# Threshold attention into an ELU feed-forward block: idle transposes and step order in the first stage, and the place of the weight conversion in the second

## The chip, the core and the metric

The kernel runs on one core of one Trainium2 chip. The metric is the device time of one execution in microseconds. The kernel before takes 1376.89 us, the median of three runs (1376.81 to 1378.41).

A core has five engines that work side by side, each through its own list of instructions in order, and wait for one another by semaphores: TensorE (PE in the profile; its weight loads are shown apart as PEld), VectorE (DVE), ScalarE (ACT), GpSimd (POOL) and SyncE (SP), which issues the transfers. TensorE writes its results to PSUM; the operands of the others lie in SBUF or PSUM.

## What is computed

Attention with a threshold, for 8 sequences of 8 heads with 576 positions of 64 numbers, and behind it a feed-forward block with the ELU function:

```python
scores = scale * np.matmul(q, k.transpose(0, 1, 3, 2))
thresh = np.max(scores, axis=-1, keepdims=True) - tau
scores = np.where(scores >= thresh, scores, -1000000000.0)
scores = scores - np.max(scores, axis=-1, keepdims=True)
attn = np.exp(scores)
attn = attn / (np.sum(attn, axis=-1, keepdims=True) + 1e-09)
x = np.matmul(attn, v)            # then heads side by side: 4608 x 512
h = x @ w_in                      # 512 -> 2048
g = np.where(h > 0.0, h, np.exp(np.minimum(h, 0.0)) - 1.0)
return g @ w_out                  # 2048 -> 512
```

q, k and v come as 32-bit numbers. The two weight matrices come as 64-bit numbers, and the kernel turns them into 32-bit ones itself, from the two 32-bit halves of each.

## The kernel before

**Steps.** Two heads make a pair; a sequence has four pairs, and the kernel 32. A pair is worked in five steps i = 0 to 4. Steps 0 to 3 each take 128 query rows of both heads; step 4 takes the last 64 rows of both heads as one block of 128. Steps are numbered through as n: n = 0 to 19 are the first sequence, and n = 20 begins the second.

**One step.** TensorE makes the scores of a head as two products of 288 columns (line 236, tile `sc`). VectorE takes the maximum of each row (276 in the first stage, 246 in the second, `mx`). From it come the exponential's bias `nb` and the threshold `th`, small operations on GpSimd and in part on ScalarE. ScalarE takes the exponential (287, 251, `e`). VectorE masks, that is it multiplies the exponential by the comparison with the threshold and sums the row (296, 263, `w`); a reciprocal of the sum follows (`rs`), and GpSimd normalizes `w` (272). TensorE transposes `w` in blocks of 128 columns (306, `rt`), ScalarE copies the transposed blocks to SBUF (322, `wTa`, `wTb`), and after two or three steps TensorE multiplies them with v (416, 420, `pv`).

**Three stages.** The first stage is the first sequence (n below 20): there is no feed-forward work yet. The second (n = 20 to 34) adds the first sequence's feed-forward work in halves of a unit, and converts what is left of the weights. The third (n from 35) has the rest, with the feed-forward products placed by a planner with costs and due times; the change does not touch it. In the first two stages the order of the instructions on each engine is that in which the program text issues them, but the build moves some: the first conversion of n = 20 stands, on VectorE and GpSimd, ahead of the mask and the second head's normalization of n = 17, and one rescaling on ScalarE as well.

**First stage, order within a step.** `turn_parts` returns the transposes of the step before as parts: two sets of four blocks and, for the middle columns that both share, a last one. In a usual step the first part stands on TensorE behind this step's scores, and the second before the next step's scores, which are issued one step ahead; the last part stands behind them. In steps with i = 2 or 4, and n not 0, the next scores go first, and all parts follow them (`first_scores`). Scores have three buffers in this stage, so that the second head's next scores wait for this step's first mask.

**Idle transposes.** Before a part, `room` issues as many transposes of the identity matrix as stand in the list `spare`; nothing reads their result. Before the loop, `idle(28)` does the same while q and k are loaded. In the usual steps of the first stage there are 6 ahead of the first part and 8 ahead of the second.

**Conversion.** A piece of weights is 128 x 512. There are 32, of which 6 end in the first stage, so that the second converts two per step in n = 20 to 32. A piece takes: `convert_rest` (126, ScalarE), `convert_top`, which is a shift (137) and a combination of sign and rest (142) on VectorE, `convert_add` (148, GpSimd), `convert_abs` (153, ScalarE) and `convert_end` (160, VectorE, behind the masks). In a step of the second stage, the first piece's `convert_top` and `convert_add` are issued ahead of the maximum, the second piece's behind it. In that stage one buffer holds the scores of both heads, so that the next scores wait for both masks. A step is "valued" where the product with v falls in it: i = 1 or 3.

Of the kernel before, what the change touches and what calls it, by code (L numbers as in the profile page):

```python
# [19 lines left out]
def kernel(  # L20
# [107 lines left out]
    def convert_top(i):  # L128
        convert_shift(i)
        convert_sign(i)  # L130


    def convert_shift(i):
        if i in staged:
            hi = staged[i][:, :, 1]
            top = tops[i] = wstage.tile([P, WN], U32, name="wtop", bufs=2)
            nc.vector.tensor_scalar(top, hi, 3, 0x3FFFFFFF, ALU.logical_shift_left, ALU.bitwise_and)  # L137

    def convert_sign(i):
        if i in staged:  # L140
            hi, top = staged[i][:, :, 1], tops[i]
            nc.vector.scalar_tensor_tensor(top, hi, 0xC0000000, top, ALU.bitwise_and, ALU.bitwise_or)  # L142

    def convert_add(i):

        if i in staged:
            top = tops[i].bitcast(I32)
            nc.gpsimd.tensor_tensor(top, top, staged[i][:, :, 0].bitcast(I32), ALU.add)  # L148
# [67 lines left out]
    spare = []  # L216
# [88 lines left out]
    def transpose(dst, src):  # L305
        nc.tensor.matmul(dst, src, ident, is_transpose=True, skip_group_check=True)  # L306
# [221 lines left out]
    NB = NC + 1  # L528
    steps = [(pr, i) for pr in range(NP) for i in range(NB)]
    per_seq = NPAIR * NB  # L530
# [35 lines left out]
    def finish_units(after, engines):  # L566
        for posts in after:
            for post in posts[engines]:
                post()
# [3 lines left out]
    with tc.manual_schedule():  # L573
        load(0, ("qm",))
        nc.sync.dma_start(tau_sb, tau.to_broadcast([P, 1]))
        load(0, ("km",), queue=nc.scalar)
        load(0, ("v",))
        load(1)


        def idle(n):
            rt = psum["t"].tile([P, NC, P], FP32, name="rt", tag="rt")
            for _ in range(n):
                transpose(rt[:, 0], ident)

        idle(28)
        prep_q(0)
        prep_k(0)
        read_tau()
        copy_k(0)  # L590
        copy_q(0)
        scores(0, 0, [0, 1])
        out_values = None
        for n in range(per_seq):
            pr, i = steps[n]
            hs = heads_of(i)
            x = progress[1]
            if n:
                normalize(*steps[n - 1], [0])
                turned = turn_parts(*steps[n - 1])  # L600
            max_of(pr, i, 0)
            exp_of(pr, i, 0)
            bound_of(pr, i, 0)
            if n and i not in (2, NB - 1):
                spare.append(6)
                copies = turned[0]()
            if len(hs) == 2:
                max_of(pr, i, 1)
                st = open_steps[pr, i]
                nc.gpsimd.tensor_scalar(st["nb"][:, 1:], st["mx"][:, 1:], nkeep, 1.0, ALU.mult, ALU.mult)  # L610
            if n and len(heads_of(steps[n - 1][1])) == 2:
                normalize(*steps[n - 1], [1])
            if len(hs) == 2:
                exp_of(pr, i, 1, True)
                bound_of(pr, i, 1)
            if out_values:
                out_values()
            if n and i not in (2, NB - 1):
                copies()

            if i == NB - 1 and n + 1 < per_seq:
                convert_top(x)
                convert_add(x)
                convert_abs(x)
                convert_rest(x + 1)
            elif i == 0 and n:
                convert_end(x)
                load_w()
            elif i == 1 and pr:
                convert_sign(x)  # L630
                convert_add(x)
            elif i in (2, 3):
                (prep_q if i == 2 else prep_k)(pr + 1)
                (copy_q if i == 2 else copy_k)(pr + 1)
            mask_of(pr, i, 0)

            first_scores = bool(n) and i in (2, NB - 1)
            if n and not first_scores:
                spare.append(8)
                turned[1]()()  # L640
            if n + 1 < per_seq:
                scores(*steps[n + 1], heads_of(steps[n + 1][1]))
            if n:
                for part in turned[0 if first_scores else 2 :]:
                    part()()
            if len(hs) == 2:
                mask_of(pr, i, 1)
            reciprocal_of(pr, i, hs)
            out_values = None
            if n > 1 and steps[n - 2][1] in (1, NB - 1):  # L650
                out_values = values(steps[n - 2][0], 0 if steps[n - 2][1] == 1 else 1)
            if i == 0 and n:
                convert_shift(x + 1)
            elif i == 2 and pr:
                convert_end(x)
                load_w()
            if i == 1 and pr:
                convert_abs(x)
            if i == 2 and n + 3 < per_seq:
                convert_rest(progress[1])  # L660
            if i in (3, 4):
                load(pr + 2, ("qm",) if i == 3 else ("km",))
            if i == 3 and pr:
                load(pr + 1, ("v",))
            if n == 0:
                load_w()
                load_w()
        for h in heads_of(steps[per_seq - 1][1]):
            normalize(*steps[per_seq - 1], [h])
# [11 lines left out]
    with tc.manual_schedule():  # L681
        carried = []
        for _ in range(2):
            load_w(4)
        for n in range(per_seq, SWITCH):
            pr, i = step = steps[n]
            hs = heads_of(i)
            now = range(progress[1], min(progress[1] + 2, len(pieces)))
            if n == per_seq:
                for x in now:  # L690
                    convert_rest(x)
            for _ in now:
                load_w(4)
            scores(*step, hs)
            valued = steps[n - 2][1] in (1, NB - 1)
            if valued:
                out_values = values(steps[n - 2][0], 0 if steps[n - 2][1] == 1 else 1)
            parts = turn_parts(*steps[n - 1])
            for x in now[:1]:
                convert_top(x)  # L700
            finish_units(carried, slice(0, 2))
            for x in now[:1]:
                convert_add(x)
            copies = parts[0]()
            if not valued:
                copies()
            exponentials(*step, hs)
            finish_units(carried, slice(2, None))
            if valued:
                out_values()  # L710
                copies()
            for x in now[:1]:
                convert_abs(x)
            share = SHARES[n % NB]
            after = ffn_halves(share[0])
            finish_units(after, ACT)
            for x in now[1:]:
                convert_top(x)
                convert_add(x)
                convert_abs(x)  # L720
            parts[1]()()
            second = ffn_halves(share[1])
            finish_units(second, ACT)
            if len(parts) > 2:
                parts[2]()()
            carried = ffn_halves(share[2])
            masks(*step, hs)
            finish_units(after + second, slice(1, 2))
            for x in now:
                convert_end(x)  # L730
            finish_units(after + second, slice(2, None))
            normalize(*step, hs)
            if i in (2, 3):
                (prep_q if i == 2 else prep_k)(pr + 1)
                (copy_q if i == 2 else copy_k)(pr + 1)
            if i in (3, 4):
                load(pr + 2, ("qm",) if i == 3 else ("km",))
            if i == 3:
                load(pr + 1, ("v",))
            if steps[n - 2] == (NPAIR - 1, NB - 1):  # L740
                push_ffn(0)
            for x in range(progress[1], min(progress[1] + 2, progress[0])):
                convert_rest(x)
        finish_units(carried, ALL)
        turn(*steps[SWITCH - 1])
        finish_units(ffn_halves(len(pending)), ALL)
        behind(*steps[SWITCH - 2])
        behind(*steps[SWITCH - 1])
# [87 lines left out]
    with tc.manual_schedule():  # L836
        after = []
        make_out(1), make_out(0)
        for n in range(SWITCH, MIDDLE):
            pr, i = steps[n]  # L840
# [44 lines left out]
        agenda, clock, now, serial = [], [0.0], [0.0], [0]  # L885
# [330 lines left out]
        for n in range(MIDDLE, len(steps) + 3):  # L1216
            pr, i = divmod(n, NB)
            if n <= len(steps) + 1:
                at(clock[0] + 1.5, lambda n=n: fetch(*steps[n - 2]))
            if 0 < n - MIDDLE < 4:  # L1220
                x = n - MIDDLE - 1
# [112 lines left out]
```

## Time and profile before

| what | before |
|---|---|
| time, median of 3 | 1376.89 us |
| time of the profiled run, and its span | 1375.69 us, 1373.7 us |
| VectorE / GpSimd / ScalarE busy, share of the span | 77% / 60% / 46% |
| TensorE's granted clock, mean | 0.994 |
| maxima of n = 0, 1, 2, 3, 4, 5 begin at | 9.29, 13.24, 18.91, 22.83, 29.64, 33.22 us |
| maxima of n = 5 to 10, the second pair | 33.22, 38.55, 43.32, 48.03, 53.17, 56.71 us |
| maxima of n = 17, 18, 19, 20 | 90.56, 96.55, 101.47, 107.19 us |
| maxima of n = 20, 21, 22, 23, 24 | 107.19, 115.74, 124.39, 133.49, 142.98 us |

The page of a profile gives busy time by engine first, and then the span in 40 slices. A row of the windows view gives a stretch in us from the span's start, its length, the busy time and number of instructions of PE, PEld, DVE, ACT and POOL, then the clock that TensorE was granted, the share of the transfer engines and GB/s. A row of the timeline gives start, duration, engine, line, operation, what is written and read, the number of merged instructions, and in brackets how long the engine had been idle and what ended that. The chain of waits goes back from what ended last, at each step to what released it: a row is a start, a duration and the work. A maximum's start is a good mark of a step, since it waits for the scores, and everything else in the step waits for it.

### The profile page before, as it was taken

To read this page: it belongs to the slowest core of one execution; us is meant where nothing else is said; L and a number is where in the kernel's file an instruction comes from. 1 tells how busy PE (TensorE), PEld (TensorE's weight loads), DVE (VectorE), ACT (ScalarE), POOL (GpSimd) and SP (SyncE) were. 2 spreads that over 40 slices of the span, in tenths; PEclk is the share of its full clock that TensorE was granted. 3 is DMA by queue.
4 is the path that set the end of the run, shared out by engine and by line. 5 is a ranking of instruction groups with operands and counts; after the bars stand their busy time and mean duration, and the time that the engine had idled before them with its cause. 6 is when DMAs were issued, how large, how long until landed. Compare 5 with 4: busy or idle time off the path is not lost.

```text
span 1373.7 us, 22245 instructions
## 1 busy us (share of the span) xinstructions
PE 1335.3 (97%) x6748; PEld 1003.5 (73%) x6748; DVE 1061.3 (77%) x2332; ACT 630.3 (46%) x1391; POOL 829.7 (60%) x1325
## 2 busy tenths in 40 slices
PE   7997989999999999999999999999999999999998
PEld 6664745746777777777777777777777777888886
DVE  5887885988878987888798878888888875545433
ACT  4775655325454544545453636363535442312320
POOL 4666774878647574757475647675575646525423
PEclk9999999999999999999999999999999999999999
DMA  5244452589898889798988888888889785411211
GB/s 115 59 96 138 141 148 44 183 237 260 235 256 230 250 223 267 223 260 234 250 229 246 242 245 243 217 258 220 238 234 275 220 246 167 125 67 66 92 58 31
DMA packets 316342, 259.83 MB, mean 189 GB/s; under 512 B 208320, under 2 KB 272320, under 8 KB 316224
## 3 DMA queue, kind: packets, MB, share of 16 engines
q1 hardware_dynamic: 313856, 258.13, 67.5%
q8 instruction: 54, 0.88, 0.3%
q10 hardware_dynamic: 2368, 0.30, 0.2%
q14 instruction: 64, 0.52, 0.1%
HBM read 167.84 MB, written 90.51 MB: 188 GB/s over the span
## 4 chain that ended last, share of the span: by engine, by line
PE 83%; DVE 7%; POOL 4%; ACT 3%; issue 2%; DMA 1%; SPq 0%; ACTq 0%; DVEq 0%; POOLq 0%
PE f L1091 27%; PE f L936 26%; PE sc L236 12%; PE pv L420 9%; PE rt L306 3%; PE pv L416 2%; PE f L467 2%; PE f L507 2%; DVE w L263 1%; ACT e L251 1%; DVE wtop L142 1%; POOL w L272 1%; POOL wtop L148 1%; DVE wtop L137 1%; DVE mx L276 1%
## 5 line engine op out<-in xcount | busy, mean ns | idle before, releaser
L272 POOL TENSOR_SCALAR w<-w,rs 128x576 f32<-128x576 f32 x288 | 247.6, 864 | 125.8 <-DVE rs L303 95.1
L276 DVE TENSOR_REDUCE mx<-sc 128x1 f32<-128x576 f32 x243 | 173.6, 751 | 85.7 <-PE sc L236 85.7
L296 DVE SCALAR_TENSOR_TENSOR w<-sc,th,e 128x576 f32<-128x576 f32 x243 | 191.6, 811 | 20.8 <-ACT e L287 6.5
L287 ACT ACTIVATE e<-sc,nb,keep 128x576 f32<-128x576 f32 x243 | 200.6, 831 | 8.3 <-POOL nb L610 0.7
L380 DVE STREAM_TRANSPOSE x<-w 128x512 f32<-128x512 f32 (+1 forms) x350 | 182.6, 568 | 8.2 <-POOL w L272 8.2
L285 ACT ACTIVATE nb<-mx,nkeep 128x1 f32<-128x1 f32 x227 | 67.3, 297 | 247.0 <-DVE mx L276 247.0
L236 PE MATMUL sc<-kT,qT 64*128 64x288 f32 x1024 | 164.0, 432 | 15.0 <-DVE w L263 9.1
L236 PEld LDWEIGHTS sc<-kT,qT 64*128 64x128 f32 x1024 | 91.0, 187 | 76.5 <-issue 51.8
L280 POOL TENSOR_SCALAR th<-mx,ntau 128x1 f32<-128x1 f32 x243 | 64.5, 266 | 112.0 <-DVE mx L276 111.2
L936 PE MATMUL f<-xt,sw 128*128 128x256 f32 x512 | 128.8, 389 | 0.5 <-DVE g L958 0.5
L936 PE MATMUL f<-xt,w_in_sb 128*128 128x256 f32 x512 | 124.6, 382 | 0.4 <-ACT w L950 0.2
L936 PEld LDWEIGHTS f<-xt,sw 128*128 128x128 f32 x512 | 93.3, 190 | 28.9 <-issue 13.5
L936 PEld LDWEIGHTS f<-xt,w_in_sb 128*128 128x128 f32 x512 | 96.0, 190 | 19.3 <-ACT xs L432 4.6
L1091 PE MATMUL f<-w_out_sb,s 128*128 128x256 f32 x448 | 109.4, 387 | 0.0
L1091 PE MATMUL f<-w_out_sb,g 128*128 128x256 f32 x448 | 107.6, 382 | 0.5 <-DVE g L991 0.5
L1091 PE MATMUL f<-t,s 128*128 128x256 f32 x448 | 106.6, 380 | 0.3 <-POOL s L1028 0.3
L936 PE MATMUL f<-x,w_in_sb 128*128 128x256 f32 x448 | 105.8, 379 | 0.0
L1091 PEld LDWEIGHTS f<-w_out_sb,s 128*128 128x128 f32 x448 | 82.3, 190 | 23.0 <-issue 11.3
L1091 PEld LDWEIGHTS f<-w_out_sb,g 128*128 128x128 f32 x448 | 83.8, 190 | 16.9 <-issue 3.8
L955 POOL TENSOR_TENSOR u<-u,w 128x256 f32<-128x256 f32 x64 | 49.0, 765 | 76.5 <-ACT u L950 76.5
L1091 PEld LDWEIGHTS f<-t,s 128*128 128x128 f32 x448 | 84.1, 190 | 13.7 <-POOL s L1028 2.7
L936 PEld LDWEIGHTS f<-x,w_in_sb 128*128 128x128 f32 x448 | 85.1, 190 | 11.6
(165 smaller groups left out, 2499.6 us busy)
## 6 DMA issues: line engine op xcount, KB each, us to landing
there<-x SPq DMA_DIRECT2D x500, 144.0 KB, 4.3
wTb<-there SPq DMA_DIRECT2D x75, 576.0 KB, 4.9
wTa<-there SPq DMA_DIRECT2D x50, 576.0 KB, 4.4
sw<-win_sums SPq DMA_DIRECT2D x62, 384.0 KB, 4.7
t<-wout_sums SPq DMA_DIRECT2D x45, 512.0 KB, 5.4
qm<-in_q_dram SPq DMA_DIRECT2D x128, 72.0 KB, 4.5
vm<-in_v_dram SPq DMA_DIRECT2D x64, 128.0 KB, 4.2
wst<-in_moe_w_in_dram SPq DMA_DIRECT2D x16, 512.0 KB, 4.4
```

Of the source, the lines that this page charges most:

```text
L236: nc.tensor.matmul(scs[h][:, a, :HALF], qs[r], kT[r, k0 : k0 + HALF], start=True, stop=True)
L272: nc.gpsimd.tensor_scalar(wv, wv, st["rs"][:, h : h + 1], 1.0, ALU.mult, ALU.mult)
L276: nc.vector.tensor_reduce(st["mx"][:, h : h + 1], st[h][:, :, :HALF], axis=AX.XY, op=ALU.max)
L280: nc.gpsimd.tensor_scalar(st["th"][:, h : h + 1], st["mx"][:, h : h + 1], 1.0, ntau, ALU.mult, ALU.add)
L285: nc.scalar.mul(st["nb"][:, h : h + 1], st["mx"][:, h : h + 1], nkeep)
L287: nc.scalar.activation(e, st[h][:, :, :HALF], AF.Exp, bias=st["nb"][:, h : h + 1], scale=keep)
L296: nc.vector.scalar_tensor_tensor(wv, sc[:, :, :HALF], st["th"][:, h : h + 1], e, ALU.is_ge, ALU.mult, accum_out=st["sm"][:, h : h + 1])
L380: nc.vector.transpose(x[:, :, c0 : c0 + nc_], src.rearrange("p (c g n) -> p g c n", c=nc_, n=T))
L420: nc.tensor.matmul(pv[h * D : (h + 1) * D, g0 * T : g1 * T], vm[:, h, c], wT[:, g0:g1, h * (NC + 1) + c], start=False, stop=(c == NC - 1), ...
L936: nc.tensor.matmul(loc["banks"][place], left[:, j], right[:, j], start=(begins and j == 0), stop=(j == 1), skip_group_check=True)
L955: nc.gpsimd.tensor_tensor(loc[name], x(), loc[other], op)
L1091: nc.tensor.matmul(place(m), lhs, rhs, start=(begins and v == 0), stop=(v == RU - 1), skip_group_check=True)
```

## The change

It has two parts. In the first stage, the first pair of heads gets more idle transposes: 16 in step 0, which had none, and 9 and 11 instead of 6 and 8 in its later usual steps; and its step i = 2 takes the usual order, since `first_scores` asks for n > 2 now. These are to keep TensorE at work while the pair has no other work for it. In the second stage, the first piece's conversion is issued behind the maximum, and behind the carried work of the feed-forward part, in the valued steps and in n = 20; in the others it stays ahead of it. This is to let the maximum start as soon as the scores are there. With it, the first conversion of n = 20 no longer stands in n = 17; the rescaling on ScalarE still does.

```diff
-            if n and i not in (2, NB - 1):
-                spare.append(6)
+
+            first_scores = n > 2 and i in (2, NB - 1)
+            if n and not first_scores:
+                spare.append(6 if pr else 9)
                 copies = turned[0]()
...
-            if n and i not in (2, NB - 1):
+            if n and not first_scores:
                 copies()
...
             mask_of(pr, i, 0)
-
-            first_scores = bool(n) and i in (2, NB - 1)
             if n and not first_scores:
-                spare.append(8)
+                spare.append(8 if pr else 11)
                 turned[1]()()
+            elif not n:
+                idle(16)
             if n + 1 < per_seq:
                 scores(*steps[n + 1], heads_of(steps[n + 1][1]))
...
             parts = turn_parts(*steps[n - 1])
-            for x in now[:1]:
-                convert_top(x)
+
+            behind_max = valued or n == per_seq
+            if not behind_max:
+                for x in now[:1]:
+                    convert_top(x)
             finish_units(carried, slice(0, 2))
-            for x in now[:1]:
-                convert_add(x)
+            if not behind_max:
+                for x in now[:1]:
+                    convert_add(x)
             copies = parts[0]()
             if not valued:
                 copies()
             exponentials(*step, hs)
             finish_units(carried, slice(2, None))
+            if behind_max:
+                for x in now[:1]:
+                    convert_top(x)
+                    convert_add(x)
             if valued:
                 out_values()
                 copies()
```

## The prediction, on record before the result

> **What bounds the kernel now.** The page comes first:
>
> ```profile
> PE 1335.3 (97%) x6748; PEld 1003.5 (73%) x6748; DVE 1061.3 (77%) x2332; ACT 630.3 (46%) x1391; POOL 829.7 (60%) x1325
> ```
>
> TensorE bounds the whole, but the change touches only steps 0 to 31, which end near 207 us. What is saved there moves the PE-full rest (217 us on) forward whole. I therefore read the early part: the windows view cut at the changes of the granted clock, TensorE's timeline, then the chain of waits.
>
> ```profile
> 9.94:13.36 3.42, 1.03 (x6) 0.70 (x6) 2.70 (x9) 1.85 (x3) 0.78 (x3) 1.00 0.84 144
> 13.36:16.77 3.41, 3.41 (x16) 3.26 (x16) 2.78 (x6) 2.44 (x4) 2.23 (x5) 0.50 0.70 165
> ...
> 20.18:23.60 3.42, 1.77 (x12) 1.29 (x13) 3.35 (x10) 1.40 (x2) 2.12 (x6) 1.00 0.39 64
> 23.60:27.00 3.40, 3.10 (x15) 2.50 (x14) 1.41 (x3) 3.10 (x7) 1.97 (x6) 0.50 0.43 68
> ...
> 108.93:112.34 3.41, 0.00 (x0) 0.00 (x0) 2.28 (x6) 3.26 (x8) 2.09 (x3) 1.00 0.00 1
> 112.34:115.76 3.42, 3.34 (x10) 1.76 (x10) 3.35 (x7) 1.01 (x2) 2.40 (x2) 0.50 0.38 89
> ```
>
> Second number: PE busy; third from the end: granted clock. Three 3.41 us windows run at half clock, each behind a window in which PE was busy 1.03, 1.77 and 0.00 us. The window 6.53 to 9.94, with 2.38 busy (70%), was followed by full clock: the limit lies between 52% and 70%.
>
> ```profile
> 12.33 1.25 PE L236 MATMUL sc<-kT,qT 64*128 64x288 f32 x6 [2.59 <-DVE w L296]
> 13.52 1.54 PE L306 MATMUL rt<-ident 128*128 128x128 f32 x6
> ...
> 17.64 1.24 PE L236 MATMUL sc<-kT,qT 64*128 64x288 f32 x8
> ...
> 21.82 1.24 PE L236 MATMUL sc<-kT,qT 64*128 64x288 f32 x6 [2.01 <-DVE w L296]
> ...
> 25.09 1.54 PE L306 MATMUL rt<-ident 128*128 128x128 f32 x6 [0.30 <-ACT wTa L322]
> ...
> 27.16 1.04 PE L306 MATMUL rt<-ident 128*128 128x128 f32 x8
> 28.03 0.60 PE L306 MATMUL rt<-ident,w 128*128 128x128 f32 x4
> 28.47 1.14 PE L236 MATMUL sc<-kT,qd 128*128 128x288 f32 x4
> ```
>
> Scores of steps 1 to 4 begin at 12.33, 17.64, 21.82 and 28.47; PE idles 2.59 and 2.01 us for the masks; six idle transposes take 1.54 us when cold (0.257 each), and eight warm ones hold PE from 27.16 to 28.03, 0.109 each.
>
> The second piece is one vector chain:
>
> ```profile
> 92.59 0.74 DVE L137 TENSOR_SCALAR wtop<-wst 128x512 uint32<-128x512 uint32 x1
> 93.37 0.69 DVE L142 SCALAR_TENSOR_TENSOR wtop<-wst,wtop 128x512 uint32<-128x512 uint32 x1
> 93.98 0.81 DVE L296 SCALAR_TENSOR_TENSOR w<-sc,th,e 128x576 f32<-128x576 f32 x1
> ```
>
> This is the timeline of VectorE, and next the chain of waits in order of time:
>
> ```profile
> 114.71 0.57 DVE wtop L142
> 115.27 0.68 issue
> 115.95 1.29 POOL wtop L148
> 117.24 0.43 POOL nb L247
> ```
>
> Step 20's first conversion in fact runs in step 17, ahead of its mask. In step 21 the conversion and its POOL addition stand in the chain ahead of `nb`. The chain, by line from 107 to 142 us, is ACT exponentials 17.8%, masks 13.5% and conversions (L137, L142, L148, L160) some 30%; PE is only 2% of it through its transposes.
>
> **What the Trainium skill says.** (1) "TensorE: Matmul & The Clock Gate", Part 1: the clock halves after an idle window of about 3.4 us and recovers after a busy one. The trace agrees: 3.41. (2) The same page, Part 4, says that transposes do not count as activity. The trace disagrees: PE did nothing but 28 idle transposes from 1.46 on, and the clock record opens at full rate at 6.53. The measurement decides. (3) "SBUF — State Buffer", Who interferes with whom: VectorE and GpSimd share a port pair under an exclusive lock; a two-port op, or one with two SBUF inputs, and a GpSimd op block each other for a whole instruction. The trace agrees: L142 has minimum, median and maximum 0.691, 0.692 and 1.115 us, and is long where a normalization waited behind L137:
>
> ```profile
> 158.34 0.42 DVE L137 TENSOR_SCALAR wtop<-wst 128x512 uint32<-128x512 uint32 x1
> 158.79 1.11 DVE L142 SCALAR_TENSOR_TENSOR wtop<-wst,wtop 128x512 uint32<-128x512 uint32 x1
> ```
>
> **Part 1: transposes and order, steps 0 to 4.** The 16 new ones fill the 2.59 us gap: PE has done scores 0 at 9.27, 16 x 0.109 is 1.7, so they end near 11.1, ahead of the mask at 12.2. Scores 1 stay at 12.33. The window 9.94 to 13.36 then holds about 2.2 to 2.8 us of work (over 63%): no cold stretch. Warm, from 13.55: 9 idle, 4 real, 11 idle, 4 real, 28 x 0.109 = 3.05: scores 2 at 16.6 instead of 17.64, its mask (over at 16.1) being in time. Step 2 in the usual order: scores end 17.9, 0.2 for the one transpose left over, again 3.05: scores 3 at 21.2 instead of 21.82. The second head's normalization (20.66 before, now about 19.7 to 20.45) and the mask (20.04 to 20.86) are in time, and the 2.01 us gap is filled. Step 3 loses the eight real transposes and copy waits that followed scores 3 (22.99 to 25.09): 22.4 + 0.2 + 3.05 gives scores 4 at 25.7 instead of 28.47. From there 3.48 us of PE work (values among it) leads to step 5 as before. **Gain 2.8 us**, in which the 32 more idle transposes of steps 1 to 3 (6, 20, 6) are paid with 32 x 0.109 = 3.5; bounds 1.4 (cold stretches placed kindly in other runs of before) and 3.6.
>
> **Part 2: step 17 without the conversion.** The mask waits for the exponential (first half over near 93.15) and the second transpose, not for L142: 93.2 instead of 93.98. The scalar rescaling at 91.74 stays. **Gain 0.8**; the third pair's like step took 4.72 between maxima (66.81 to 71.53), this one 5.99 (90.56 to 96.55), so at most 1.27.
>
> **Part 3: conversions behind the maxima, steps 20, 21, 23, 26, 28, 31** (the valued ones while the 32 pieces last). The order per engine is now: max, L137, L142, L137, L142, mask on DVE; `nb`, `th`, two L148, normalizations on POOL. Without contention two pairs are 2 x 1.11 = 2.2 us, just what lies between maximum and mask (108.55 to 110.71). But the first addition is ready when the first L142 ends and waits while the second L137 runs; then, as at 158.79, it gets the port ahead of the second L142. I take that: L148's 1.29, less a start of 0.1, blocks; mask at maximum end + 3.25 instead of + 2.16 to 2.27. Lower end: no blocking, + 2.2. Upper: + 3.5.
> - Step 20: the conversion removed from step 17 lands here: -1.1 (0 to -1.3). Queued behind the mask: scores 21.
> - Step 21: maximum from 115.74 to about 114.75, when cold scores end (+1.0), less 1.1: 0.
> - Step 23: maximum 132.46 instead of 133.49; `nb` earlier by 1.15; +0.15, and up to 0.5 because TensorE waited 1.73 for ACT's `xt` copy there. Step 28 alike: +0.15. Both: 0.5.
> - Step 26: PE is full from 150 to 166.9: 0. Its mask would move 0.7 later, but scores 27 wait for PE until 166.65 anyway.
> - Step 31: maximum from 203.65 to 202.0: 1.65 - 1.1 = +0.6.
>
> Together 0.0. ScalarE's magnitude of the second piece waits for the second L142, but has over 1 us of slack ahead of L160. Sum: 2.8 + 0.8 + 0.0 = 3.6; timed runs of before are about 1 us above its profiled run (1375.69), which suggests their cold stretches were no kinder, so 0.2 more: 1376.9 - 3.8 = **1373.1**.
>
> **Rivals.**
> - No port blocking: part 3 gives 0 + 1.0 + 1.1 + 0 + 1.1 + 1.65 = 4.9 and the sum is 8.5: **1368.4**. For: L142 is undisturbed next to small `th`. Against: L148 is long and L142 is at 1.11 behind each delayed normalization.
> - The wait moves: masks at + 3.5, which takes 0.25 more in five steps, and kind cold stretches before: 1.4 + 0.8 - 1.3 = 0.9, so **1376.0**, no change. For: every conversion only changes place, and step 20 gains one.
> - Transposes do not keep the clock: the cold windows stay, 32 additional ones at up to 0.257 cost 8.2, less the 2.0 us gap they fill, the 2.1 of copy waits and real transposes gone after scores 3, and part 2's 0.8: + 3.3, **1380.2**, slower. Against: point (2).
>
> **Chances.** Forecast 0.6 (spread about 1 us), no blocking 0.18, moved wait 0.17, cold 0.05. The range 1369.5 to 1376.0 leaves out the cold case and most of the no-blocking one, about 0.2. Under 1374.1 (0.2%): 0.18 and most of 0.6, some 0.69; above 1379.6: 0.05; the rest 0.26.
>
> **What would show it.** Right: full clock from 6.5 us to the gap at step 20; scores 2, 3, 4 at 16.6, 21.2, 25.7; mask 17 right after the exponential; L142 at about 1.7 to 1.9 us once in each of the six steps. Wrong: a half-clock window before 30 us, L142 at 0.69 throughout (faster), or step 21 starting later than 1 us behind its forecast.

## The result and the profile after

The changed kernel takes 1370.24 us (median of 4 runs, 1369.7 to 1371.45), the kernel before 1377.65 us beside it (4 runs, 1376.81 to 1379.33): a ratio of 0.9946, interval [0.9929, 0.9963], or 7.4 us less. The forecast was 1373.1 us, 3.8 less. Direction and range held; the gain is about twice the forecast.

| | before | after |
|---|---|---|
| profiled run, and its span | 1375.69, 1373.7 us | 1370.03, 1368.3 us |
| maximum of n = 5 begins at | 33.22 us | 30.32 us |
| maxima of n = 17, 18 | 90.56, 96.55 us | 87.66, 92.80 us |
| maxima of n = 20, 21, 22 | 107.19, 115.74, 124.39 us | 103.60, 112.15, 121.73 us |
| maxima of n = 30, 31, 32 | 194.90, 203.65, 212.39 us | 191.75, 198.55, 208.15 us |
| maximum of n = 35 | 239.84 us | 235.59 us |

The page's busy times, as before, tell little:

```profile
PE 1335.0 (98%) x6796; PEld 1005.3 (73%) x6796; DVE 1063.7 (78%) x2332; ACT 630.8 (46%) x1391; POOL 827.6 (60%) x1325
```

There are 48 more instructions on TensorE (16 new idle transposes and 32 from the larger counts and the new order), and yet its busy time is the same: they fill gaps, and other work beside them now runs at full clock. The windows view shows it (second number: TensorE busy; third from the end: granted clock):

```profile
9.42:12.83 3.41, 3.29 (x23) 2.52 (x23) 2.76 (x5) 1.85 (x3) 0.78 (x3) 1.00 0.84 135
12.83:16.25 3.42, 3.42 (x30) 2.98 (x28) 2.72 (x9) 2.19 (x4) 2.23 (x5) 1.00 0.68 164
16.25:19.66 3.41, 3.41 (x30) 2.76 (x29) 2.64 (x7) 1.86 (x5) 1.20 (x3) 1.00 0.63 232
...
104.17:107.58 3.41, 0.20 (x2) 0.00 (x0) 3.34 (x5) 2.75 (x5) 2.46 (x3) 1.00 0.25 103
107.58:110.99 3.41, 1.17 (x6) 0.98 (x8) 3.34 (x9) 2.31 (x6) 2.07 (x3) 0.50 0.00 0
110.99:114.41 3.42, 3.42 (x12) 1.29 (x10) 2.53 (x4) 0.40 (x1) 2.37 (x4) 0.50 0.70 201
```

Where before had 1.03 us of work and then half clock, there are now 3.29 us and full clock. The one half-clock stretch left, but for the last us of the run, is the forecast one behind the gap of step 20; it lasts two windows, where before had one there. TensorE's timeline gives the starts of scores 1 to 4:

```profile
9.57 1.97 PE L306 MATMUL rt<-ident 128*128 128x128 f32 x16
11.47 2.08 PE L236 MATMUL sc<-kT,qT 64*128 64x288 f32 x8
13.48 1.20 PE L306 MATMUL rt<-ident 128*128 128x128 f32 x9
...
16.68 1.24 PE L236 MATMUL sc<-kT,qT 64*128 64x288 f32 x8
...
21.17 1.24 PE L236 MATMUL sc<-kT,qT 64*128 64x288 f32 x8
...
25.56 1.14 PE L236 MATMUL sc<-kT,qd 128*128 128x288 f32 x4
```

The sixteen stand where 2.59 us were idle, and scores 2, 3 and 4 begin at 16.68, 21.17 and 25.56 (forecast 16.6, 21.2, 25.7). Next, VectorE's timeline in step 17, where the conversion is gone and the mask begins 2.67 us behind the maximum's start, not 3.42. The line names GpSimd's normalization, over at 90.15; the first exponential (89.41, 0.83) was over last, at 90.24:

```profile
87.66 1.42 DVE L276 TENSOR_REDUCE mx<-sc 128x1 f32<-128x576 f32 x2 [0.18 <-PE sc L236]
89.00 0.77 DVE L192 STREAM_TRANSPOSE qT<-qm 128x576 f32<-128x576 f32 x1
90.33 0.82 DVE L296 SCALAR_TENSOR_TENSOR w<-sc,th,e 128x576 f32<-128x576 f32 x1 [0.56 <-POOL w L272]
```

Last, the timeline of all engines in step 20, where that conversion has gone; VectorE's two lines of before come first, then the changed kernel's:

```profile
107.19 1.36 DVE L246 TENSOR_REDUCE mx<-sc 128x2 f32<-128x1152 f32 x1 [2.48 <-PE sc L236]
...
110.71 0.82 DVE L263 SCALAR_TENSOR_TENSOR w<-sc,th,e 128x576 f32<-128x576 f32 x1 [1.09 <-ACT e L251]
```

```profile
103.60 1.36 DVE L246 TENSOR_REDUCE mx<-sc 128x2 f32<-128x1152 f32 x1 [2.53 <-PE sc L236]
...
105.33 0.69 DVE L142 SCALAR_TENSOR_TENSOR wtop<-wst,wtop 128x512 uint32<-128x512 uint32 x1
...
105.94 0.42 DVE L137 TENSOR_SCALAR wtop<-wst 128x512 uint32<-128x512 uint32 x1
106.37 1.28 POOL L148 TENSOR_TENSOR wtop<-wtop,wst 128x512 int32<-128x512 int32 x1
106.39 1.81 DVE L142 SCALAR_TENSOR_TENSOR wtop<-wst,wtop 128x512 uint32<-128x512 uint32 x1
...
108.13 0.81 DVE L263 SCALAR_TENSOR_TENSOR w<-sc,th,e 128x576 f32<-128x576 f32 x1
```

The addition L148 comes in at 106.37, just behind the second L137 and behind `th`, which GpSimd had begun at 105.41 and ended at 106.40. The second L142 takes 1.81 us instead of 0.69. The mask starts at the maximum's end (104.96) + 3.17; before it was + 2.16, and the forecast was + 3.25. In the six changed steps the second L142 takes 1.66 to 1.83. In step 21's part of the chain of waits the addition is no longer ahead of the exponentials; what stands there is VectorE alone (`issue` is time for which the chain shows no cause; here it is the rest of the second L142, which takes 1.82 us from 114.94 in the timeline):

```profile
114.94 0.68 DVE wtop L142
115.61 1.07 issue
116.68 1.56 DVE w L263 x4
```

**Where the trace gained**, from the starts of the maxima: 2.90 us by step 5; 0.85 from step 17 to 18; 0.16 lost by step 20; 0.93 lost from 20 to 22; 0.25 gained in each of steps 23 and 28 (+1.02 ahead of the maximum, -0.77 behind it); nothing in step 26 (+0.79, -0.79); 1.10 in step 31 (+1.95, -0.85). That is 4.25 by step 35, where the last edit is past. The third stage adds about 1.15, to the 5.4 by which the spans differ, though no edit lies there. A single wait in the trace of before, in TensorE's timeline of the third stage, carries most of that:

```profile
925.96 0.67 PE L416 MATMUL pv<-wTa,vd 128*128 128x256 f32 x2 [1.19 <-DMA wTa<-there]
```

At this place (steps 130 and 131) the lead grows by 1.42 us; from step 35 to 129 it had stayed between 3.88 and 4.73. It is a transfer that came late in that run: the unedited kernel's second trace, shown below, gains 1.43 on the first one at the same two steps. The changed kernel's largest wait on this transfer is 0.2.

### The profile page after: what moved, and what is told of

It is laid out like the page before. It is cut to its first block, busy times and chain, and to the rows that moved or that the text cites. A ratio compares the mean times of both kernels' runs of the same rounds, so it can differ in the third digit from the quotient of the medians.

```text
span 1368.3 us, 22345 instructions
## 1 busy us (share of the span) xinstructions
PE 1335.0 (98%) x6796; PEld 1005.3 (73%) x6796; DVE 1063.7 (78%) x2332; ACT 630.8 (46%) x1391; POOL 827.6 (60%) x1325
## 4 chain that ended last, share of the span: by engine, by line
PE 86%; DVE 5%; POOL 3%; issue 2%; ACT 2%; DMA 1%; SPq 0%; ACTq 0%; DVEq 0%; POOLq 0%
PE f L1101 28%; PE f L946 27%; PE sc L236 12%; PE pv L420 9%; PE rt L306 3%; PE pv L416 2%; PE f L467 2%; PE f L507 2%; DVE w L263 1%; DVE wtop L142 1%; POOL w L272 1%; ACT e L251 1%; DVE wtop L137 1%; POOL wtop L148 1%; DVE mx L246 1%
## 5 line engine op out<-in xcount | busy, mean ns | idle before, releaser
L1101 PEld LDWEIGHTS f<-w_out_sb,s 128*128 128x128 f32 x448 | 82.3, 190 | 23.0 <-issue 11.3
```

Of the source, the lines that this page charges most:

```text
L1101: nc.tensor.matmul(place(m), lhs, rhs, start=(begins and v == 0), stop=(v == RU - 1), skip_group_check=True)
```

## Experiments

The runs were made in four sets. Each of the three below was made on another chip, and the kernel before had medians of 1376.89, 1376.77 and 1379.96 us in them. A gain is against before in the same set, by the ratio; a comparison across sets is called that.

### Theory and rivals

Theory: A, the whole first-stage edit works by leaving no window of 3.41 us with too little work; B, step 17 gains 0.85 and step 20 pays it back; C, the addition of GpSimd gets between L137 and the second L142 and costs about 0.77 of what the later conversion could gain. Rivals: the idle transposes or the order would do the first stage alone; the second stage brings nothing; the conversions are slow for another reason.

### First stage alone, second stage alone, and before once more

The changed kernel with the conversion issued as before; and the kernel before with only the conversion edit.

```diff
-            behind_max = valued or n == per_seq
-            if not behind_max:
-                for x in now[:1]:
-                    convert_top(x)
+            for x in now[:1]:
+                convert_top(x)
...
```

> The first stage of the changed kernel (16 idle transposes in step 0, 9 and 11 in the first pair, usual order in step 2) with the second stage of the kernel before. Theory A (clock and gaps): no half-clock window before 30 us, scores of steps 2, 3, 4 near 16.7, 21.2 and 25.6 us, the maximum of step 5 at 30.3 instead of 33.2, the first conversion of step 20 still in step 17. The trace is 2.9 us shorter; the timed gain is 2.9 to 5, because runs of before whose clock windows fall otherwise (1376.8 to 1379.3 against 1375.7 for the profiled one) lose more than the profiled run did. Rival B (the first stage gives only its 2.9 us, and the larger timed gain comes from the second stage): 2.4 to 3.2 us in the timed runs. Rival C (only the order counts): as A in the trace, told apart by the runs of its parts.

Measured: 1372.47 us (1371.82 to 1373.07), ratio 0.9969 [0.9957, 0.998], by that 4.3 us less. Step 5 begins 2.91 us earlier, step 18 still 2.82, and full clock reaches from 5.34 to 107.7 us. The conversion edit plays no part in the first 2.9. At the last step this trace is 4.1 us ahead, 1.42 of it at steps 130 and 131.

> The second stage of the changed kernel with the first stage of the kernel before: cold windows near 13.4 and 23.6 us stay. Theory A: step 17 0.85 us shorter, step 20 about 0.95 longer, step 21 +1.0, step 31 near +1.9 less 0.9 behind it, together 1.3 us by step 35; in time 1.3 to 2.5 us with what the third stage adds. Rival B: 4 us or more in time. Theory of the port lock: the second L142 of steps 20, 21, 23, 28 and 31 takes 1.8 us, its first 0.69.

Measured: 1376.0 us (1372.83 to 1378.31), ratio 0.9989 [0.9978, 1.0]: by that 1.5 us less, or nothing. Its maxima show each step of the second stage as in the changed kernel: +0.83 (17 to 18), -0.94 (21 to 22), +1.03 and -0.78 (22 to 24), +1.95 (30 to 31). Its second L142 takes 1.67 to 1.82 us in the six steps. But its first stage, the same instructions as before, was 1.60 us slower in this trace by step 4. The windows view says why:

```profile
9.12:12.53 3.41, 0.81 (x7) 0.39 (x6) 2.62 (x5) 1.85 (x3) 0.78 (x3) 1.00 0.87 140
12.53:15.94 3.41, 3.41 (x14) 2.43 (x13) 2.62 (x7) 1.55 (x3) 1.74 (x4) 0.50 0.64 141
...
22.77:26.19 3.42, 3.04 (x13) 2.18 (x12) 2.13 (x4) 1.66 (x4) 2.47 (x6) 0.50 0.45 73
26.19:29.60 3.41, 3.41 (x18) 3.41 (x17) 1.90 (x6) 2.56 (x5) 0.00 (x0) 0.50 0.81 168
```

The windows begin 0.83 us earlier than in the trace of before (12.53 against 13.36), and the second half-clock stretch lasts two windows instead of one. Where the windows fall differs from run to run, and with it what a gap costs.

> The kernel before, unchanged, for a second trace and as a measure of what two equal kernels differ by. Theory A (the clock's windows run free of the kernel): half-clock windows of 3.41 us stand at other places than 13.4 and 23.6 us, still one or two before 30 us, and step 5 begins between 32 and 35 us; the third stage differs by about 1 us from the first trace without any edit. Rival (the windows start with the kernel): the same places within 0.1 us, and times all alike. Ratio within 0.2% of 1.

Measured: 1376.87 us (1375.29 to 1383.9), ratio 1.0006 [0.9992, 1.0021]. Its half-clock windows stood 0.34 us earlier (13.02 and 23.26), one each as in before, and step 5 began within 0.03 us; at step 21 it had two windows where before had one, and lost 0.45. Without any edit this trace is 0.92 us behind that of before at step 35 and 0.49 ahead at step 151. So of two traces, differences up to about 1.4 us in stages without an edit are the runs' own.

### The halves of the first-stage edit

The transposes without the order of step 2, the order with the old counts and without the sixteen, and the whole but for the sixteen (all three with the conversion as before):

```diff
-            first_scores = n > 2 and i in (2, NB - 1)
+            first_scores = n > 0 and i in (2, NB - 1)      # transposes alone
...
-                spare.append(6 if pr else 9)
+                spare.append(6)                            # order alone; so too 8, and no idle(16)
...
-            elif not n:
-                idle(16)                                   # no sixteen
```

> First stage: only the additional transposes (16 in step 0, 9 and 11 in steps 1 and 3), the order of step 2 as before. Second stage as before. Clock theory with gaps: no half-clock window near 13 us, scores 2 near 16.7; scores 3 go out first behind a gap of 2 us and begin near 20.9; behind it a half-clock window comes or not, by where the 3.41 us windows fall: scores 4 at 26.7 without, at 28.7 with it. So 0 to 1.8 us shorter than before in the trace, about 1 to 2.5 in time. Rival (the transposes bring the gain): 2.5 us or more, as in the whole first stage.

> First stage: only the order of step 2 is the changed one; no transposes in step 0, and 6 and 8 elsewhere, as before. Second stage as before. Clock theory with gaps: the gap behind scores 0 stays, so one half-clock window near 13 us stays and scores 2 begin near 17.6; the gap ahead of scores 3 is filled by step 2's own transposes (scores 3 near 21.8), so the second half-clock window goes and scores 4 come near 25.9 instead of 28.5: the trace is about 2.5 us shorter, in time 2 to 4 us. Rival (the transposes, not the order, bring the gain): under 1 us, with both windows still there.

> First stage as changed, but without the 16 transposes of step 0. Second stage as before. Clock theory: the gap behind scores 0 is back, a half-clock window stands near 13 us, and the 20 idle transposes of step 1 run in it at 0.2 us and more each: scores 2 near 18.4 instead of 16.7, all later steps 1.7 us later than in the whole first stage; 1.2 us of gain left in the trace. Rival (the clock has nothing to do with the gap, the transposes only cost): scores 2 at 16.7 without half clock, the time that of the whole first stage.

| kernel | us (lowest to highest) | ratio | step 5 in its trace |
|---|---|---|---|
| transposes alone | 1377.39 (1372.97 to 1383.94) | 1.0001 [0.9985, 1.0017] | 1.29 later |
| order alone | 1375.69 (1372.07 to 1377.69) | 0.999 [0.9978, 1.0001] | 2.02 earlier |
| no sixteen | 1375.95 (1374.64 to 1379.35) | 0.999 [0.9977, 1.0002] | 0.25 later |
| whole first stage | 1372.47 (1371.82 to 1373.07) | 0.9969 [0.9957, 0.998] | 2.91 earlier |

No half has a gain clear of the noise; the whole has 4.3 us, and the smallest spread. In its trace the order alone did keep 2.02 of the 2.91 us at step 5; it was 0.4 ahead at the end, and 1.9 us of waits for late transfers stand in its third stage. The clock was recorded in every timed run: its mean was 0.9940 in before (this set), 0.9947 with the order alone, 0.9949 without the sixteen, 0.9954 with the transposes alone, and 0.9962 with the whole (beside 0.9944 before in its set). So each half took away a part of the half-clock time, and the whole the most, but the time doesn't follow the clock alone. The windows views show the gap that each left. First the transposes alone, whose step 2 still waits for its mask (1.82 us of work, then two windows at half clock), then the one without the sixteen (1.09, then two windows):

```profile
17.21:20.62 3.41, 1.82 (x11) 0.81 (x7) 2.67 (x6) 2.27 (x5) 2.00 (x5) 1.00 0.46 178
20.62:24.03 3.41, 2.99 (x10) 1.95 (x11) 2.87 (x8) 0.18 (x1) 1.67 (x5) 0.50 0.54 87
24.03:27.45 3.42, 3.04 (x14) 2.53 (x13) 0.78 (x2) 2.74 (x6) 1.48 (x4) 0.50 0.39 64
```

```profile
8.65:12.06 3.41, 1.09 (x9) 0.63 (x6) 2.16 (x4) 1.85 (x3) 1.02 (x4) 1.00 0.85 137
12.06:15.47 3.41, 3.14 (x11) 2.15 (x12) 2.71 (x8) 0.94 (x2) 1.01 (x2) 0.50 0.64 132
15.47:18.89 3.42, 3.42 (x18) 3.42 (x17) 1.98 (x6) 1.60 (x3) 1.99 (x4) 0.50 0.83 287
```

In the second, the additional idle transposes themselves run at half clock, and scores 2 begin at 19.84 (18.4 was expected; 17.64 before): idle transposes behind a gap cost, in the gap they pay. In all eight traces with the sixteen no half-clock window begins before 20 us; in all five without, one begins between 12.06 and 13.36 us. The order alone met one half-clock window (13.31 to 16.72) and put scores 2, 3 and 4 at 17.71, 22.12 and 26.44, each within 0.55 of what was expected.

### What blocks the second L142

All shifts ahead of the combinations in the six steps, so that no addition has its input while a shift runs; then the same for every converting step.

```diff
             if behind_max:
+                for x in now:
+                    convert_shift(x)
+                for x in now:
+                    convert_sign(x)
                 for x in now[:1]:
-                    convert_top(x)
                     convert_add(x)
...
             for x in now[1:]:
-                convert_top(x)
+                if not behind_max:
+                    convert_top(x)
```

> The changed kernel, but in the six steps whose conversion stands behind the maximum VectorE does both shifts (L137) first and then both combinations (L142), so that the first addition on GpSimd becomes ready only while the second L142 already runs. Port-lock theory: no L142 over 0.8 us in these steps, the mask begins 2.2 to 2.4 us behind the end of the maximum instead of 3.3, 0.9 to 1.1 us earlier in steps 20, 21, 23, 28 and 31 (step 26 is bound by TensorE); 4 to 5 us faster than the changed kernel, near 1365.5. Rival (the second L142 waits for something of its own, a buffer or the addition itself): it still takes 1.8 us, and the time is that of the changed kernel within 1 us.

Measured: 1368.25 us (1368.15 to 1370.6), ratio 0.9943 [0.9931, 0.9954]: across sets 2.0 us below the changed kernel's median, though hardly below its ratio (0.9946), where 4 to 5 us were expected. The time doesn't show the gain, so the steps have to. The timeline in step 20:

```profile
105.08 0.75 DVE L137 TENSOR_SCALAR wtop<-wst 128x512 uint32<-128x512 uint32 x2
105.33 0.55 POOL L247 TENSOR_SCALAR nb<-mx,nkeep 128x2 f32<-128x2 f32 x1 [3.09 <-DVE mx L246]
105.75 1.29 DVE L142 SCALAR_TENSOR_TENSOR wtop<-wst,wtop 128x512 uint32<-128x512 uint32 x2
105.87 1.22 POOL L248 TENSOR_SCALAR th<-mx,ntau 128x2 f32<-128x2 f32 x1
105.92 1.55 ACT L251 ACTIVATE e<-sc,nb,keep 128x576 f32<-128x576 f32 x2 [0.87 <-POOL nb L247]
...
107.57 0.82 DVE L263 SCALAR_TENSOR_TENSOR w<-sc,th,e 128x576 f32<-128x576 f32 x1 [0.54 <-ACT e L251]
```

Both L142 together take 1.29: the blocking is gone, as the theory says. The mask stands at maximum end + 2.40 instead of + 3.17, and now waits for the exponential, because `nb` takes 0.55 behind two shifts in a row (0.30 in the changed kernel). Against the changed kernel's trace the step ends 0.74, 0.53 and 0.45 us earlier in steps 20, 23 and 28. Step 26 gains nothing, since TensorE is full there, and step 31 lost 0.82 to a half-clock window (196.8 to 200.2) that the other trace didn't have. Step 21 gained only 0.04: its mask stood 0.75 nearer, but VectorE then sat idle for 0.75 us ahead of L160, waiting for the magnitude (L153), which stands behind both additions. The expectation counted five steps at 0.9 to 1.1.

```diff
-            behind_max = valued or n == per_seq
+            behind_max = True
```

> The changed kernel with the shifts ahead of the combinations, as in the run before, and the conversion behind the maximum in all thirteen steps of the second stage that have one. If the conversion ahead of the maximum is what delays steps 22, 27, 29, 30 and 32 as it delayed 21 and 31, the maxima there come 1.2 to 1.7 us earlier (step 29 only 0.5, since one head's exponential leaves too little room); steps 24 and 25 are bound by TensorE: 4 to 6 us faster than the shifts-first kernel, near 1363.5. Rival (those steps are held by the feed-forward work): within 1.5 us of 1368.3.

Measured: 1365.47 us (1364.17 to 1366.2), ratio 0.9916 [0.9901, 0.9932]. This version beats both kernels, by 11.3 us the one before and, across sets, by 4.8 us the changed one. All 32 L142 take 0.675 to 0.693 us here. What the conversion ahead of the maximum still cost in the other steps is given back there; the 1363.5 expected was missed by 2.

### Step 20 put back, the gap of step 20 filled, and fewer idle transposes

The first of these three is the changed kernel with one line changed; the other two build on the version with every conversion behind the maximum.

```diff
-            behind_max = valued or n == per_seq
+            behind_max = valued                            # step 20 as before
```

> The changed kernel, but in step 20 the first conversion stands ahead of the maximum again, as before the change (it stays behind in the valued steps 21, 23, 26, 28, 31). It is then moved into step 17 again, ahead of its mask. THEORY: the interval from the maximum of step 17 to that of step 18 is 0.85 us longer than in the changed kernel (5.99 instead of 5.14), and the mask of step 20 stands 1.0 us nearer to its maximum (+2.2 instead of +3.17), so the two cancel: total 1370.1 to 1370.6, equal to the changed kernel. RIVAL (step 20 was no loss, since step 21 waits for something else): 0.8 us slower than the changed kernel, 1371.0.

Measured: 1370.98 us (1368.99 to 1372.79), ratio 0.9939 [0.9922, 0.9957]. The time can't separate the theories, but the steps can: 0.84 later from 17 to 18, 1.00 regained from 20 to 21, 0.08 behind at step 23. Point B is confirmed, to about 0.1 us: what step 17 gained, step 20 paid.

```diff
             for x in range(progress[1], min(progress[1] + 2, progress[0])):
                 convert_rest(x)
+            if n == per_seq:
+                idle(36)
```

> The version with every conversion behind the maxima (1365.47 us), and 36 more idle transposes at the end of step 20, behind the real transposes of step 19 (over at 104.4 us) and ahead of the scores of step 21 (109.08 to 111.37 at half clock, behind a gap of 4.71 us). CLOCK THEORY (idle transposes hold the clock wherever they stand): 36 x 0.109 = 3.9 us fill the gap to about 108.5 to 109.0, no half-clock window behind it, scores 21 take 1.24 instead of 2.29 and end near 110.3. The maximum of step 21 then waits for the two conversion ends on VectorE (over at 110.83): it begins at about 110.9 instead of 111.40, 0.5 us earlier; total 1364.5 to 1365.0, ratio to before about 0.9912. RIVAL 1 (idle transposes work only at the start, while nothing else ran): half-clock window near 109 stays, time 1365.5. RIVAL 2 (the idle ones get their buffer late and hold the scores up): scores 21 begin after 109.5, time 1365.5 to 1366.5.

TensorE's timeline and the windows view of this kernel:

```profile
104.96 4.15 PE L306 MATMUL rt<-ident 128*128 128x128 f32 x36 [0.52 <-ACT wTb L322]
109.06 1.24 PE L236 MATMUL sc<-kT,qT 64*128 64x288 f32 x8
```

```profile
104.40:107.80 3.40, 2.88 (x27) 2.85 (x27) 2.86 (x6) 2.52 (x5) 2.61 (x3) 1.00 0.26 102
107.80:111.20 3.40, 3.40 (x24) 2.19 (x24) 3.33 (x9) 2.34 (x7) 2.98 (x3) 1.00 0.00 0
```

Scores 21 take 1.24 instead of 2.29, no half clock is left until the last 3 us of the run, and the maximum of step 21 starts at 110.84 (expected 110.9), 0.63 us nearer to step 20's than without. That is the sharpest test of the clock theory: idle transposes hold the clock in the middle of the kernel too. All six timed runs had a mean clock of 0.999 or 1.0, against 0.996 to 0.999 without the thirty-six. Over all, 1365.54 us (1363.81 to 1370.7), ratio 0.9898 [0.9871, 0.9926], is not separable from the version without. Its profiled run, 1370.7, was the slowest of six: 0.59 ahead at step 35, it lost 7 us in the third stage. TensorE's waits for transfers from 240 us on (total, number, longest):

```profile
PE pv L416 <- DMA wTa<-there: 3.8, 5, 1.7
...
PE f L952 <- DMA sw<-win_sums: 0.6, 1, 0.6
...
PE pv L416 <- DMA there<-x: 0.3, 1, 0.3
```

The trace of the version without it has none of these transfer waits, and these add to 4.7 us of the 7 lost. They are late transfers as in before at 925.96; why they come late in some runs wasn't tried.

```diff
-                spare.append(6 if pr else 9)
+                spare.append(6)
...
-                spare.append(8 if pr else 11)
+                spare.append(8)
```

> The version with every conversion behind the maxima, in which the first pair keeps the sixteen of step 0 and the usual order of step 2, but has 6 and 8 idle transposes in its usual steps again instead of 9 and 11. Question: are these six more per step needed. CLOCK THEORY with the limit between 52% and 70%: with six fewer (0.65 us) in a step of 4.5 us TensorE is still busy over 80%, so the clock stays full; scores 2 follow the mask of step 1 (over at 16.1 us) at about 16.1 instead of 16.7, scores 3 at about 20.2 to 20.5 instead of 21.2, scores 4 at about 24.3 to 24.8 instead of 25.6: step 5 starts 0.6 to 1.3 us earlier, total 1364.2 to 1364.9. RIVAL (the additional ones are what keeps the clock): a half-clock window of 3.41 us between 12 and 30 us, step 5 starts 0 to 2 us later, total 1365.5 to 1367.5.

Measured: 1368.05 us (1363.93 to 1374.23), ratio 0.9922 [0.9892, 0.9951]. The clock stayed full to 107.7 us, so the counts of 9 and 11 are not what keeps it. Scores 3 and 4 came at 21.00 and 25.31 (this run is 0.27 later from its start), later than expected, because their transposes then wait for a normalization:

```profile
20.41 0.66 PE L306 MATMUL rt<-ident,w 128*128 128x128 f32 x4 [0.36 <-POOL w L272]
21.00 1.24 PE L236 MATMUL sc<-kT,qT 64*128 64x288 f32 x8
```

Step 5 came 0.49 us nearer to step 1. The lead was lost again at step 21, 0.86, where this run had two half-clock windows (6.83 us) behind the gap and the version with 9 and 11 had one. The time expected (1364.2 to 1364.9) was missed.

## Why the prediction was right, and where its size was off

- **Part 1, forecast 2.8, measured 2.90 in the trace.** The sixteen fill the gap, the windows stay full, and scores 2, 3 and 4 are within 0.15 us of the forecast. The bounds held. The additional transposes were paid as computed; one trace adds that six fewer per step would have done.
- **The Trainium skill on the clock.** "TensorE: Matmul & The Clock Gate", Part 4, says that full clock doesn't engage for transposes, which don't count as busy in the same way. The sixteen, and the 36 at step 20, show that here they count. Part 1's window of about 3.4 us is borne out by every stretch (3.41, or 6.83 for two).
- **"The limit lies between 52% and 70%"** fails in the same trace of before, further on: a window with 1.68 us of work (49%) was followed by full clock.

```profile
180.61:184.02 3.41, 1.68 (x8) 0.72 (x7) 2.27 (x5) 2.78 (x6) 2.61 (x4) 1.00 1.27 173
184.02:187.44 3.42, 3.40 (x14) 1.89 (x13) 3.32 (x9) 2.66 (x7) 2.40 (x2) 1.00 0.28 58
```

- **Part 2, forecast 0.8, measured 0.85.** The mask of step 17 follows the exponential and not L142.
- **Part 3, forecast 0.0, measured +0.50 by step 35** (with 0.16 lost between steps 18 and 20). Blocking by the addition, from "SBUF — State Buffer", Who interferes with whom, was the right mechanism: + 3.17 against + 3.25, and it vanished when the shifts went first. In one detail it was otherwise: what waited while the shift ran was `th` (105.41 to 106.40), and the addition came behind `th`. Steps 20 and 21 together gave -0.93 for -1.1; steps 23 and 28 +0.50 for 0.5; step 26 nothing, as forecast. **Step 31 was mis-sized**: 1.10 for 0.6. Its maximum came 1.95 earlier instead of 1.65, since before ran that step's scores partly at half clock (1.58 us) and the changed kernel at full (1.24), and its mask cost 0.85, not 1.1. The prediction counted three half-clock windows and left this fourth one of before out:

```profile
197.67:201.09 3.42, 1.51 (x10) 0.95 (x10) 2.41 (x8) 3.40 (x9) 1.63 (x2) 1.00 0.00 0
201.09:204.50 3.41, 3.41 (x10) 1.05 (x9) 3.38 (x5) 0.18 (x1) 2.64 (x3) 0.50 0.64 191
```

- **"3.6 moves the rest forward whole"**: 4.25 did, to within 0.5 up to step 129, and a late transfer in the trace of before added 1.42 at steps 130 and 131. The forecast took the rest of that trace for a fixed length; the control shows that it isn't.
- **The allowance of 0.2 for the timed runs was the largest miss, and its cause stays open.** The medians differ by 7.4 us, the profiled runs by 5.66: 1.75 is left that the traces don't hold. The profiled run of before (1375.69) lay 1.96 below the median of before in that set, that of after 0.21 below its own. That timed runs of before lose more to half-clock windows than its profiled run did doesn't fit the clock that was recorded with them: in 80 timed runs of before, in the three sets above, its mean was 0.994 (0.991 to 0.996), as in the profiled run. A part may be the draw of four runs, since two sets of 28 and 35 runs of before had medians 0.8 to 0.9 lower than that set's 1377.65. Late transfers are a rival, as one trace waited 4.7 us for them; the timed runs have no trace to tell.
- **Luck.** By its steps the forecast was close: 4.25 for 3.6. That the range held is the mechanism's doing; that the total came so near its lower end is not, since no term foresaw the late transfer (1.42) or the 1.75.
- **Rivals.** The time, 1370.24, is nearer to "no port blocking" (1368.4) than to the forecast; L142 at 1.66 to 1.83 us in every changed step refutes that rival's mechanism all the same. The step times decide, not the total. "The wait moves" is partly true: in steps 21, 23, 26, 28 and 31 the mask gives back 0.77 to 0.93 us of the 0.79 to 1.95 that the maximum gained. "Transposes don't keep the clock" fell.

## What to carry to other kernels

A gap on TensorE costs more than its length, because up to two windows of work behind it run at half clock; fill all gaps of such a stretch or expect little, since with a single one left over no gain clear of the noise remained, and in two of three traces none at all by step 5. When work is moved behind a reduction, look at what another engine will slip between its instructions: like operations side by side (both shifts, then both combinations) avoided the blocking here. And compare step times, not only totals: one profiled run is a draw from runs that differ by some us without an edit.

## What the runs showed of the hardware that was not expected

- How much work in a 3.41 us window keeps the clock, over all thirteen traces, from the first entry of each clock record on: windows at full clock with up to 1.52 us of TensorE's work (44%) were always followed by half clock, those with 1.86 us (54%) or more always by full. Between them both happened: 1.77 (before, 20.18) and 1.82 us (transposes alone, 17.21) were followed by half clock, 1.68 (before, 180.61) and 1.72 us (fewer idle transposes, 5.26) by full. At half clock, windows with 2.99 to 3.14 us of work were followed by a second one in three traces, but 3.04 and 3.10 also by full clock; 2.87 us (84%) and less always by a second one, 3.23 us (95%) and more never. Some records can be missing, so what decides in between stays open.
- Between a shift and a combination GpSimd's addition got in (106.37, and L142 took 1.81). With two combinations in a row nothing of GpSimd did: the `th` that began at 105.87, in the first, ended at 107.09, just behind the second. Whether the addition would have waited likewise isn't shown, since it stood behind `th`.
- Transfers in the third stage, whose instructions were the same, kept TensorE waiting by 1.19 us in the trace of before, by 4.7 us over seven waits in one other, and not at all in a third.
